# Attention and a gated feed-forward layer on one core: other costs in the kernel's own scheduler, loads held behind stores, and normalisations moved in pairs

## The chip, the cores and the metric

The kernel runs on one core of one Trainium2 chip. The metric is the device time of one execution in microseconds; the time of a kernel is the median of its runs. The engines are named as in the profile: PE (TensorE, matmuls), ACT (ScalarE), DVE (VectorE), POOL (GpSimd) and SP (SyncE). POOL and SP issue all the DMAs here: POOL the loads, SP the stores and the DMA transposes.

## The reference

Two steps, one behind the other. Inputs and output are float32.

```
k_proj = E @ k;  v_proj = F @ v            # per batch and head: 64 x 1024 times 1024 x 64
attn   = softmax(q @ k_proj.T / sqrt(64))  # 1024 x 64, over the 64 projected keys
x      = attn @ v_proj                     # 8 batches, 8 heads, 1024 tokens, 64 wide
x      = heads side by side                # 8192 tokens x 512
out    = (sigmoid(x @ w_gate) * (x @ w_val)) @ w_out   # 512 -> 1536 -> 512
```

## The kernel before

**Work.** A batch has 1024 tokens, and a block is half of that: 512 tokens, so there are 16 blocks. In a block the feed-forward layer runs in three units K (K = 3 times the block, plus 0 to 2), each over four of the twelve column groups of 128. Most matmuls are 128x128 by 256 columns in bf16: from block 1 on, products are taken by a scheme with seven instead of eight half-size products (the names S1 to S4 and T1 to T4 are its sums of activations and of weights). Sums of activations are made by `xs_sums` (L1627, out of xT) and `s_sums` (L1361, out of hT), sums of weights by `vt_sums` (L1555), `gt_sums` and `t_sums`. All these sums run on DVE.

**Buffers.** Eight PSUM banks (F0 to F3, A0 to A3). In SBUF there is one buffer for q of a batch (`Qb`), one for k and v (`KVs`), one for the turned q (`qT`), two for the turned attention output (`xT0`, `xT1`, by turns), two for the gated activations (`hT0`, `hT1`) and one for output rows (`ost`, four tiles of 128 rows). A buffer is used again as soon as its readers are done.

**Attention.** For batches 0 and 1 it is done with PE transposes and with softmax sums spread by matmuls. `bc2(R)` in batch 0 multiplies such spread reciprocals in PSUM, and the two normalisations behind it (`scale`, L825, on DVE) write the tokens of block 1 into xT. From batch 2 on, `head` (L1188) works on one head: scores, exponentials on ACT, the product with v, and `normal` on DVE. After every second head SP issues a DMA transpose of the pair into xT (L1217). q is turned in the same way into qT (L882, `transpose_q`), and the projected keys into kpB (L933). Each of these is a `DMA_TRANSPOSE` of SP.

**Order by hand.** Batch 0 (until about 86 us in the profile) is written out by hand: a list `todo` of PE steps, and extra pieces hung behind step i with `put(i, ...)` or, for the four parts of the later list, with `on(u, j, ...)`, which is `put(11 + 9u + j, ...)`. Steps 1 to 10 are the `mstep`s of block 0, four matmuls of 512 columns for the gate and four for the value, with a tanh on ACT and `gate` (L1287, its product is L1294) on DVE. Steps 11 and 13 are `g_step`s of block 1, step 12 (`p1`) and step 14 (`p26`) are its value products.

**Order by a scheduler.** All that follows (blocks 2 to 15, and with it batches 2 to 7 of the attention) is first noted as tasks and then put in order by `arranged` (L53). It goes through the tasks on a clock of its own. A task is ready when its predecessors are done by the counts of `COST` (L28): `busy` is how long a task keeps its engine, `lat` is how long until its result is there. Of the ready tasks of an engine, the one with the earliest due time (`rank`) goes first. The order it finds is the order in which each engine's queue holds its instructions; on the chip every engine then works through its queue strictly in that order, and stops at the first instruction whose semaphores are not there. A DMA counts as follows (L39):

```
if self.dma:
    self.busy, self.lat = (0.85 if eng == "POOL" else 0.6), t if t is not None else 3.0
```

So a load on POOL is counted with 26.0 to landing (`load`, L397), and every DMA of SP with 0.6 at issue and 3.0 to landing. A store has a further `pad` of 3.0 on each of its predecessors (L1452).

**Dependencies.** A task names keys that it reads (`r`) and writes (`w`). A reader waits for the last writer, a writer waits for the last writer and for all readers since. The same keys give the waits on the chip (`Plan.add`, L149) and the predecessors in the scheduler. A wait for a DMA is a wait for its landing.

**Loads.** In batch b (b = 1 to 6) `next_loads(b + 3)` (L2041) issues the loads of q, k and v of batch b + 3. They read the keys `("turned", r)`, so they wait for the four xT transposes of the batch; k also waits for kpB. In program order these loads come behind the stores of block 2b - 1 and ahead of those of block 2b.

**Stores.** `o_chain` (L1459) makes the output products of one block, evicts them into `ost` (`evac`, `add_snap`), and `stored` (L1443) issues one store of 256 KB per tile: tiles 2 and 3 first, then 0 and 1. The first eviction of a block (tiles 0 and 1, by ACT) overwrites what the last two stores of the block before it read.

Of the kernel before, what the change touches and what calls it, by code (L numbers as in the profile page):

```python
# [27 lines left out]
COST = {"PE": (0.0, 0.22), "ACT": (0.52, 0.12), "DVE": (0.63, 0.12), "SP": (0.1, 0.0), "POOL": (0.85, 0.0)}  # L28


class Task:
    def __init__(self, eng, call, t):
        self.eng, self.calls, self.goal = eng, [] if call is None else [call], None
        busy, tail = COST[eng]
        self.busy = busy if t is None else t
        self.tie, self.pad = (), 0.0
        self.lat = self.busy + tail
        self.dma = call is not None and call[5] is not None
        if self.dma:  # L39
            self.busy, self.lat = (0.85 if eng == "POOL" else 0.6), t if t is not None else 3.0  # L40

    def pre_of(self, later):
        return later.pre[self.n]
# [73 lines left out]
class Plan:  # L117
# [20 lines left out]
    @contextlib.contextmanager  # L138
    def group(self, goal, us):
        if self.tasks is None:  # L140
            yield
            return
        self.open = Task("PE", None, us)
        self.open.goal = goal
        yield
        self.tasks.append(self.open)
        self.open = None
# [85 lines left out]
def bass_linformer_attn__then__ffn_glu_sigmoid_kernel(  # L233
# [18 lines left out]
    with contextlib.ExitStack() as es:  # L252

        def sbuf(name, shape, dtype):
            return es.enter_context(nc.sbuf_tensor(name, shape, dtype))
# [8 lines left out]
        def within(shape, dtype):  # L264

            n = 1
            for x in shape[1:]:
                n *= x
            if dtype == FP32:
                n *= 2  # L270
            t = early[0][:, used[0] : used[0] + n]
            used[0] += n
            if dtype == FP32:
                t = t.bitcast(FP32)
            if len(shape) == 3:
                t = t.rearrange("p (a b) -> p a b", a=shape[1])
            if len(shape) == 4:
                t = t.rearrange("p (a b c) -> p a b c", a=shape[1], b=shape[2])
            return t
# [7 lines left out]
        kp = within([P, NR, DH], BF16)  # L287
# [21 lines left out]
        qT = sbuf("qT", [P, H, 512], BF16)  # L309
        eT = sbuf("eT", [P, 8, 512], BF16)  # L310
        xu = sbuf("xu", [P, 8, 512], FP32)
        xT = [sbuf(f"xT{i}", [P, NI, 2, 512], BF16) for i in range(2)]
# [59 lines left out]
        def mm(b, o, lhsT, rhs, r, start=True, stop=True, tp=None, tr=False, read=False):  # L372
            kw = {"skip_group_check": True} if read else {}
            if tp is not None:
                kw["tile_position"] = tp
            if tr:
                kw["is_transpose"] = True
            else:
                kw["start"], kw["stop"] = start, stop
            return add("PE", lambda e: e.matmul(o, lhsT, rhs, **kw), r=r, x=[("bank", b)])  # L380

        def act(o, i, r, w, b=None, func=AF.Copy, scale=1.0, t=None):
            x = [] if b is None else [("bank", b)]
            return add("ACT", lambda e: e.activation(o, i, func, scale=scale), r=r, w=w, x=x, t=t)  # L384
# [493 lines left out]
        def transpose_q(tie=(), rs=range(NR)):  # L878
            for r in rs:
                add(  # L880
                    "SP",
                    lambda e, r=r: e.dma_start_transpose(  # L882
                        qT[:, 2 * r : 2 * r + 2, :].rearrange("p h (t c) -> p (h t) c", c=P),
                        Qb[:, 2 * r : 2 * r + 2, :].rearrange("p h c -> p (h c)"),
                    ),
                    r=[("Q", hf, r // 2) for hf in range(2)],
                    w=[("qT", r)] + [("qT", hf, r // 2, r % 2) for hf in range(2)],
                    dma=f"qT{r}",
                    tie=tie,
                )  # L890

# [60 lines left out]
        def attention(b):  # L952
# [235 lines left out]
            def head(h, goal, gap, x0, x1):  # L1188
                with group(goal, 0.215):
                    mm(x0, bank[x0][:, :], kpB[:, h, :], qT[:, h, :], ["kpB", ("qT", h // 2)])  # L1190
                act(
                    eT[:, h, :],
                    bank[x0][:, :],
                    [],
                    [("eT", h)],
                    b=x0,
                    func=AF.Exp,
                    scale=SCALE,
                )
                with group(goal + gap, 0.23):  # L1200
                    for f, bk in ((1, x0), (0, x1)):
                        for k in range(2):
                            j = 2 * f + k
                            mm(
                                bk,
                                bank[bk][:, 130 * k : 130 * k + 130],
                                eT[:, h, 128 * j : 128 * j + 128],
                                vpB[b % 2][:, h, :],
                                [("eT", h), ("vpB", b % 2, 0), ("vpB", b % 2, 1)],
                            )  # L1210
                normal(h, 1, x0)
                normal(h, 0, x1)
                if h % 2:
                    r = h // 2
                    add(
                        "SP",
                        lambda e: e.dma_start_transpose(  # L1217
                            xT[s][:, r, :, :].rearrange("p f (n c) -> p (f n) c", c=P),
                            xk[:, r, :, :, :, :].rearrange("p f g k x -> p (f g k x)"),
                        ),  # L1220
                        r=[("xk", r, c, f) for c in range(2) for f in range(2)],
                        w=[("xT", s, r, f, g) for f in range(2) for g in range(2)]
                        + [("turned", r)],
                        dma=f"xT{r}",
                    )

            return dict(
# [215 lines left out]
        def stored(blk, tts):  # L1443
            for tt in tts:
                t = 2 * (2 * (blk % 2) + tt % 2) + tt // 2
                add(
                    "SP",
                    lambda e, tt=tt, t=t: e.dma_start(out_v[blk // 2, t], ost[:, tt, :]),
                    r=[("ost", tt, n) for n in range(2)],
                    dma=f"out{tt}",  # L1450
                    t=3.0,
                    pad=3.0,  # L1452
                )
# [101 lines left out]
        def vt_sums(n, part):  # L1555
            c0, c1 = ((0, 256), (256, DFF // 2))[part]
            js = ((0,), (1, 2))[part]
            B11 = wV[:, 0:2, c0:c1]
            B12 = wV[:, 0:2, DFF // 2 + c0 : DFF // 2 + c1]
            B21 = wV[:, 2:4, c0:c1]  # L1560
            B22 = wV[:, 2:4, DFF // 2 + c0 : DFF // 2 + c1]
            T = [vT[:, k, :, c0:c1] for k in range(3)]
            o, a, b = {
                3: (T[1], B22, B12),
                1: (B12, B12, B11),
                2: (T[0], T[1], B11),
                4: (T[2], B21, T[0]),
            }[n]
            w = [("vT", n, part)]
            if n == 1:  # L1570
                w += [("wV", 3 + j, 0) for j in js]
            else:
                w += ["bsel8f", "identf", "count", "pats"]
            r = [("wV", j + k, x) for j in js for k in (0, 3) for x in range(2)]
            if n == 1:
                r = [("wV", j, 0) for j in js]
            if n == 2:
                r = [("wV", j, 0) for j in js] + [("vT", 3, part)]
            if n == 4:
                r = [("wV", j, 1) for j in js] + [("vT", 2, part)]  # L1580
            op = ALU.add if n == 2 else ALU.subtract
            dve(lambda e: e.tensor_tensor(o, a, b, op), r, w)
# [334 lines left out]
        def put(i, fn):  # L1917
            at.setdefault(i, []).append(fn)
# [4 lines left out]
        def x_sums(blk, *ns):  # L1923
            return lambda: [xs_sums(blk, n) for n in ns]
# [5 lines left out]
        qt2, sc2, den2, bc2, xo2 = half_unit(1, att)  # L1930
# [1 line left out]
        put(4, lambda: (sc2(0), sc2(1)))  # L1932
        put(4, second_loads)
        put(6, lambda: (den2(), xo2(0), xo2(1)))
        put(8, lambda: (bc2(0)(), bc2(1)()))
        put(9, x_sums(1, 1, 2))
        put(7, lambda: (vt_sums(3, 0), vt_sums(2, 0)))
        put(8, lambda: (vt_sums(4, 0), vt_sums(1, 0)))

        def own_banks():  # L1940
            FF[:] = [ffn.next() for _ in range(4)]
# [25 lines left out]
        def on(u, j, fn):  # L1967
            put(11 + 9 * u + j, fn)

        on(0, 1, x_sums(1, 3))  # L1970
        on(0, 3, x_sums(1, 4))
        on(0, 3, lambda: vt_sums(3, 1))
        on(0, 4, lambda: vt_sums(2, 1))
# [66 lines left out]

        def next_loads(b):  # L2041
            done = [("turned", r) for r in range(NR)]
            if b < B:
                load_q(b, done)
                load_k(b, ["kpB"] + done)
                load_v(b, done)
# [65 lines left out]
```

## Time and profile before

| | |
|---|---|
| median of 10 runs | 521.82 us |
| lowest and highest | 520.62 and 527.47 us |
| the profiled execution | 522.0 us, span 520.0 us |
| granted PE clock in it | 0.999 |
| PE busy | 503.9 us, 97% |
| DVE, ACT busy | 407.8 us, 78%; 349.1 us, 67% |
| loads of q, k, v (1 MB each), median to landing | 20.4, 15.5, 13.6 us |
| stores out of ost (256 KB), median to landing | 2.5 us |
| DMA transposes into qT, xT, kpB, median to landing | 3.5, 3.1, 3.2 us |

The span is the time from the first to the last instruction of the program; the time of the execution has 2.0 us more around it. Busy time is how long an engine had an instruction in it. Matmuls are pipelined, so each is shown longer than the step from one to the next. In the timelines each row has its start and its length in microseconds, the engine, the line, the operation with output and inputs, how many such instructions in a row it stands for, and in square brackets how long the engine stood idle before it and what it waited for. "SPq" is SP's queue: a row there lasts from the issue of the first to the end of the issue of the last. A landing is the time at which the DMA's semaphore is complete.

### The profile page before, as it was taken

Reading aid. Unit: us, or ns where it says so; the run is one execution under the profiler, and the core shown is the slowest. Engines: PE = TensorE matmul, PEld = TensorE weight load, DVE = VectorE, ACT = ScalarE, POOL = GpSimd, SP = SyncE. Lnnn points to the kernel's source line nnn. Section 1 sums busy time; section 2 is a strip of 40 time slices with the busy share of each in tenths; the row PEclk is TensorE's granted clock in tenths of the full one; section 3 lists DMA queues with packets and bytes.
Section 4 is the critical chain, followed back from the end, with each engine's and each line's share of the span. In section 5 each row is a group of like instructions: output and inputs, shape, how many; then the busy total and the mean of one; then the engine's idle time right before and its main releaser. Section 6 shows DMA issues by size and latency. Waiting matters only on the chain.

```text
span 520.0 us, 11316 instructions
## 1 busy us (share of the span) xinstructions
PE 503.9 (97%) x4564; PEld 409.7 (79%) x4597; DVE 407.8 (78%) x802; ACT 349.1 (67%) x650; POOL 40.4 (8%) x59
## 2 busy tenths in 40 slices
PE   5999999999999999999999999999999999999996
PEld 2544545887888788887788888888888888888885
DVE  3547789899779795987769977797968898777774
ACT  2555683878677767777667686777777766676752
POOL 9420201200200010002000020000000000000000
PEclk9999999999999999999999999999999999999999
DMA  9999999899898496546926499344104330201013
GB/s 164 199 199 204 148 201 210 122 180 222 127 228 150 107 189 112 128 83 118 219 69 122 63 169 197 82 106 88 72 1 102 42 103 1 81 2 68 14 42 122
DMA packets 105189, 63.13 MB, mean 121 GB/s; under 512 B 63025, under 2 KB 97329, under 8 KB 105137
## 3 DMA queue, kind: packets, MB, share of 16 engines
q0 software_dynamic: 33984, 29.89, 37.3%
q1 hardware_dynamic: 71152, 32.52, 28.1%
q8 instruction: 36, 0.59, 0.5%
q14 instruction: 17, 0.13, 0.1%
HBM read 60.29 MB, written 16.78 MB: 148 GB/s over the span
## 4 chain that ended last, share of the span: by engine, by line
PE 91%; DVE 3%; DMA 3%; ACT 1%; issue 1%; POOL 0%; ACTq 0%; DVEq 0%; POOLq 0%
PE pA L380 49%; PE pF L380 42%; DMA Qb<-in_q_dram 2%; DVE hT L1824 1%; DMA xT<-xu 1%; DVE vsnap L1702 1%; DVE xT L828 0%; ACT vsnap L384 0%; DVE hT L1294 0%; POOL KVs L398 0%; DVE xS L1635 0%; ACT ost L384 0%; ACT kpd L384 0%; ACT sig L384 0%; DVE gT L776 0%
## 5 line engine op out<-in xcount | busy, mean ns | idle before, releaser
L384 ACT ACTIVATE sig<-pA 128x512 f32<-128x512 f32 x126 | 75.1, 596 | 45.3 <-PE pA L380 44.8
L1691 ACT ACTIVATE pF<-pA 128x512 f32<-128x512 f32 x99 | 58.3, 589 | 30.1 <-PE pA L380 27.5
L1702 DVE TENSOR_TENSOR vsnap<-pF,vsnap 128x512 f32<-128x512 f32 x90 | 61.8, 686 | 17.5 <-ACT vsnap L384 9.6
L1778 DVE TENSOR_TENSOR sig<-pF,sig 128x512 f32<-128x512 f32 x84 | 57.6, 686 | 5.7 <-PE pA L380 2.7
L380 PE MATMUL pF<-wO,hT 128*128 128x256 bf16 (+1 forms) x400 | 59.1, 285 | 0.5 <-issue 0.2
L1824 DVE SCALAR_TENSOR_TENSOR hT<-sig,vsnap 128x512 bf16<-128x512 f32 x84 | 56.3, 685 | 1.1
L384 ACT ACTIVATE sig<-sig 128x512 f32<-128x512 f32 x84 | 52.7, 627 | 5.6 <-DVE sig L1778 5.2
L380 PE MATMUL pF<-xS,wV 128*128 128x256 bf16 x360 | 54.1, 273 | 1.2 <-DVE hT L1824 0.7
L384 ACT ACTIVATE vsnap<-pA 128x512 f32<-128x512 f32 x84 | 50.0, 596 | 7.4 <-PE pA L380 7.0
L1824 DVE SCALAR_TENSOR_TENSOR hT<-sig,pF 128x512 bf16<-128x512 f32 x42 | 28.8, 685 | 31.6 <-PE pF L380 31.5
L380 PE MATMUL pA<-xT,gT 128*128 128x256 bf16 x336 | 50.5, 273 | 1.3 <-ACT sig L384 0.9
L380 PE MATMUL pA<-xT,vT 128*128 128x256 bf16 x336 | 50.4, 273 | 0.3
L380 PE MATMUL pF<-xS,wG 128*128 128x256 bf16 x336 | 50.4, 273 | 0.0
L380 PE MATMUL pF<-xT,wG 128*128 128x256 bf16 (+1 forms) x257 | 48.9, 309 | 1.5 <-DVE hT L1294 0.8
L384 ACT ACTIVATE sig<-pF 128x512 f32<-128x512 f32 x66 | 39.5, 598 | 14.6 <-PE pF L380 13.1
L380 PE MATMUL pA<-wT,hT 128*128 128x256 bf16 x360 | 48.8, 273 | 0.0
L380 PEld LDWEIGHTS pF<-wO,hT 128*128 128x128 bf16 x402 | 38.7, 98 | 10.6 <-issue 0.8
L380 PE MATMUL pF<-xT,wV 128*128 128x256 bf16 (+1 forms) x240 | 41.5, 294 | 0.2
L380 PEld LDWEIGHTS pF<-xS,wV 128*128 128x128 bf16 x360 | 34.4, 98 | 8.2 <-DVE vsnap L1702 1.6
L380 PEld LDWEIGHTS pA<-wT,hT 128*128 128x128 bf16 x360 | 34.6, 98 | 5.1 <-ACT EF L384 0.3
L384 ACT ACTIVATE eT<-pA 128x512 bf16<-128x512 f32 x59 | 34.5, 594 | 4.8 <-PE pA L380 3.6
L380 PEld LDWEIGHTS pA<-xT,gT 128*128 128x128 bf16 x336 | 31.0, 98 | 8.4 <-issue 1.9
(162 smaller groups left out, 899.8 us busy)
## 6 DMA issues: line engine op xcount, KB each, us to landing
out_dram<-ost SPq DMA_DIRECT2D x61, 256.0 KB, 2.5
Qb<-in_q_dram POOLq DMA_DIRECT2D x7, 1024.0 KB, 20.4
KVs<-in_k_dram POOLq DMA_DIRECT2D x7, 1024.0 KB, 15.5
KVs<-in_v_dram POOLq DMA_DIRECT2D x7, 1024.0 KB, 13.6
wO<-in_moe_w_out_dram POOLq DMA_DIRECT2D x1, 1536.0 KB, 12.3
wG<-in_moe_w_gate_dram POOLq DMA_DIRECT2D x5, 256.0 KB, 18.0
wV<-in_moe_w_val_dram POOLq DMA_DIRECT2D x5, 256.0 KB, 18.6
KVs<-in_k_dram POOLq DMA_DIRECT2D x2, 512.0 KB, 8.9
```

The lines of the kernel that those rows point to most:

```text
L380: return add("PE", lambda e: e.matmul(o, lhsT, rhs, **kw), r=r, x=[("bank", b)])
L384: return add("ACT", lambda e: e.activation(o, i, func, scale=scale), r=r, w=w, x=x, t=t)
L1691: lambda e: e.activation(bank[c][:, :], bank[a][:, :], AF.Copy, scale=1.0),
L1702: lambda e: e.tensor_tensor(o, bank[bk][:, :], o, ALU.add),
L1778: dve(lambda e: e.tensor_tensor(o, bank[bk][:, :], o, ALU.add), [key], [key], b=bk)
L1824: lambda e: e.scalar_tensor_tensor(o, sg.rearrange("p (j c) -> p j c", j=2), 1.0, x.rearrange("p (j c) -> p j c", j=2), ALU.add, ALU.mult,),
```

## The change

It has four parts.

1. In the scheduler's counts a DMA transpose of SP (the keys of its semaphores begin with xT, qT or kp) keeps SP for 1.3 instead of 0.6. A transpose into qT is counted with 4.5 to landing and one into xT with `TURN = 7.0`, each instead of 3.0; the one into kpB keeps its 3.0.
2. The stores in `stored` also write a key `("stored", tt)`.
3. The loads of batches 5, 6 and 7 also read these four keys, so they wait until the stores of the block in front have landed. By the rule of the keys, the stores of the next block in turn wait for these loads.
4. In batch 0 the normalisations `bc2(0)` and `bc2(1)` no longer stand together behind step 8: the second pair stands behind step 9. The sums `x_sums(1, 1, 2)` go from step 9 to step 10, `vt_sums(1, 0)` from step 8 to step 10 and `vt_sums(4, 0)` from step 8 to `on(0, 2)`, which is step 13.

```diff
+TURN = 7.0
...
         if self.dma:
             self.busy, self.lat = (0.85 if eng == "POOL" else 0.6), t if t is not None else 3.0
+            if eng == "SP" and call[5][:2] in ("xT", "qT", "kp"):
+                self.busy = 1.3
...
                     dma=f"qT{r}",
+                    t=4.5,
                     tie=tie,
...
                         dma=f"xT{r}",
+                        t=TURN,
...
                     r=[("ost", tt, n) for n in range(2)],
+                    w=[("stored", tt)],
                     dma=f"out{tt}",
                     t=3.0,
                     pad=3.0,
...
-        put(8, lambda: (bc2(0)(), bc2(1)()))
-        put(9, x_sums(1, 1, 2))
         put(7, lambda: (vt_sums(3, 0), vt_sums(2, 0)))
-        put(8, lambda: (vt_sums(4, 0), vt_sums(1, 0)))
+        put(8, lambda: bc2(0)())
+        put(9, lambda: bc2(1)())
+        put(10, x_sums(1, 1, 2))
+        put(10, lambda: vt_sums(1, 0))
...
         on(0, 1, x_sums(1, 3))
+        on(0, 2, lambda: vt_sums(4, 0))
...
             done = [("turned", r) for r in range(NR)]
+            if b > 4:
+                done += [("stored", tt) for tt in range(4)]
             if b < B:
                 load_q(b, done)
                 load_k(b, ["kpB"] + done)
```

## The prediction

> **What bounds the kernel now.** I read the page first, then the waits of TensorE (PE), then the timelines of the engines around each wait.
>
> ```profile
> span 520.0 us, 11316 instructions
> PE 503.9 (97%) x4564; PEld 409.7 (79%) x4597; DVE 407.8 (78%) x802; ACT 349.1 (67%) x650; POOL 40.4 (8%) x59
> PE pA L380 <- DMA EF<-in_F_dram: 5.8, 1, 5.8
> PE pA L380 <- ACT sig L384: 0.9, 1, 0.9
> PE pF L380 <- DVE hT L1294: 0.8, 1, 0.8
> PE pF L380 <- DVE hT L1824: 0.7, 1, 0.7
> ```
>
> PE is the bound, and the waits name nearly all that it loses: 5.8 us at the start, which the change doesn't touch, and three single waits. Here a rule of the Trainium skill speaks against such a reading. "Perfetto Trace Analysis", section "Identifying the Most-Contended Engine", says that matmul busy share tells little of the headroom because matmuls are pipelined, and that the weight-load share tells more; by that, 79% would leave some 100 us. The trace decides against it: in the timeline of PE four matmuls of 256 columns follow each other in 0.44 us (252.68, 253.12), 0.109 us each, batch after batch, although the group table gives one 273 ns. Starts back to back leave nothing between them. So the ceiling of any reordering is the sum of the waits, not 100 us. Counted by starts, the three are a little longer than the modelled ends show:
>
> ```profile
> 46.20 1.03 PE L380 MATMUL pF<-xT,wG 128*128 128x512 bf16 x3
> 47.32 0.61 PE L380 MATMUL pF<-xT,wV 128*128 128x256 bf16 x4
> 48.72 1.04 PE L380 MATMUL pF<-xT,wG 128*128 128x512 bf16 x4 [0.78 <-DVE hT L1294]
> ...
> 42.92 0.68 DVE L1294 SCALAR_TENSOR_TENSOR hT<-sig,pF 128x512 bf16<-128x512 f32 x1
> 43.52 2.48 DVE L828 TENSOR_TENSOR xT<-pA,xu 128x512 bf16<-128x512 f32 x4
> 45.91 0.41 DVE L1582 TENSOR_TENSOR vT<-wV,vT 128x512 bf16<-128x512 bf16 x1
> 46.25 0.42 DVE L1582 TENSOR_TENSOR wV<-wV 128x512 bf16<-128x512 bf16 x1
> 46.58 0.68 DVE L1294 SCALAR_TENSOR_TENSOR hT<-sig,pF 128x512 bf16<-128x512 f32 x1
> 47.98 0.68 DVE L1294 SCALAR_TENSOR_TENSOR hT<-sig,pF 128x512 bf16<-128x512 f32 x1
> ```
>
> Wait A. Four normalisations (2.48 us) and two weight sums stand on DVE between two gates (L1294). The gates free PSUM banks F2 and F0. PE's four 512-column matmuls from 46.20 take 0.87 and the next group comes at 47.32 (0.25 lost); its four of 0.109 end at 47.76 and the next comes at 48.72 (0.96 lost). A is 1.21 us.
>
> ```profile
> 122.54 2.06 SPq L882 DMA_TRANSPOSE qT<-Qb  x1
> 124.65 1.05 SPq L1448 DMA_DIRECT2D out_dram<-ost  x2
> 125.80 4.29 SPq L882 DMA_TRANSPOSE qT<-Qb  x3
> 130.18 1.44 SPq L933 DMA_TRANSPOSE xu<-kpd  x1
> 131.67 1.33 SPq L1217 DMA_TRANSPOSE xT<-xu  x1
> 134.94 0.43 DVE L1635 TENSOR_TENSOR xS<-xT 128x512 bf16<-128x512 bf16 x1 [1.81 <-DMA xT<-xu]
> 137.15 0.61 PE L380 MATMUL pF<-xS,wV 128*128 128x256 bf16 x4 [0.73 <-DVE hT L1824]
> ```
>
> Wait B. SP issues six transposes one behind the other, 1.3 to 2.1 us each; the scheduler had counted 0.6. The last xT lands at 134.8, while DVE already stands at the sums for the next batch: 1.81 us idle, and PE starts at 137.15 instead of 135.82 + 0.44. B is 0.89 us.
>
> ```profile
> 240.74 0.88 POOL L398 DMA_DIRECT2D KVs<-in_v_dram  x1 [57.17 <-PE pF L380]
> 242.36 0.88 POOL L398 DMA_DIRECT2D KVs<-in_k_dram  x1 [0.74 <-DMA xu<-kpd]
> out_dram<-ost SPq DMA_DIRECT2D x2, 256.0 KB, 9.1
> 253.08 0.60 ACT L384 ACTIVATE ost<-pF 128x512 f32<-128x512 f32 x1 [2.24 <-PE pF L380]
> 254.22 0.61 PE L380 MATMUL pA<-xT,gT 128*128 128x256 bf16 x4 [0.94 <-ACT sig L384]
> ```
>
> Wait C. The loads of batch 6 (1 MB each) start just ahead of block 5's last stores. Those land 9.1 us after issue (the pair two us earlier, 2.4). The eviction into the same ost rows stands still until 253.08: the named PE product was done by 251, so it is the store that came last. Starts give 254.22 - 252.68 - 0.44: C is 1.10 us. The same collision at 182 and 305 (7.6 us to landing) ended just in time.
>
> **The change part by part.** No instruction is added or removed; 3.2 us are at stake.
>
> *Normalisations in pairs.* bc2(0) stays behind step 9, bc2(1) goes behind step 10; two sums go later. PE has the same matmuls, eight of the sixteen one step later. DVE after the gate of step 9 (ends 43.52): two scales at 0.62 to 44.76, gate 10 to 45.4 instead of 47.2, two scales to about 46.65, gate 11 to 47.3 instead of 48.6. p1 at 47.1 finds F2 free, the next step at 47.6 finds F0 free. New: g_step(3,0) reads the second pair for i = 2 at 46.63, and it is ready at about 46.7, so 0.1 is lost there. The moved sums (0.42 each) come at 48.0 (T1, first used after 49) and 48.8 (T4, used later), inside the 1.43 us that DVE idled before 50.42. Gain 1.21 - 0.10 = 1.1 us. What is late next is wO: issued at 58.04 behind qT transposes that the loads pace, landing 12.3 later at 70.4, first read at 71.98, then at about 70.9. Cover 0.5 us; if gone, as much of A comes back.
>
> *Longer counts.* They alter only the order in which each engine's queue holds its work from 86 us on. With 1.3 per issue and 7.0 to landing, the scheduler puts the sums of wait B behind about 138 (an issue near 131 and 7.0), which a reader can set against the landing at 134.8; before, 3.0 gave it an earlier place than the chip could keep. Their consumers, batch 2's products, start near 147. So DVE goes on with gates and B's 0.89 goes. Here a second rule speaks against the change: "Advanced Engine Details and Errata", section "X-Bar Transpose (TRN2)", has transposes as fast as other DMAs, so one count for both would do. By the rows a store alone takes 2.2 to 2.5 and an xT alone 3.1 to 3.6, nearly the rule; but with loads beside it xT took 13.2 (98 to 108 us). By the rule the 7.0 is 4 us too long in quiet stretches, B stays and the sum ends at 520.0. I side with the issue rows above, since the lateness of B is the queue's (six issues of 1.3 and more), and what the excess costs is cover: xT of a batch lands near 302, needed near 330.
>
> *Loads behind stores.* Loads of batches 5, 6, 7 begin at about 185, 246 and 308 instead of 180, 241 and 304, 4 to 5 us later. POOL's queue holds nothing else there. Last landing 22 us after the first issue: 207, 268, 330. First readers: qT transposes at 210.6, 272.5, about 333; K and V are used 50 us later. If that 3 us of cover were gone, only qT for the next batch would slip, with some 50 us to spare. Stores now land in 2.4 us, ahead of 246, the eviction needs it at 251: C's 1.10 goes.
>
> A wait is added that the title doesn't tell. ("stored", tt) is read by the loads and written by the next stores, so those of blocks 4, 6 and 8 also wait until the loads have landed. In before block 4's go at 206.6 and 214.3: in real time 0.6 us at most. But the scheduler counts 26 us per load and a pad of 3: stores out at 188, loads at 189 to 191, landed at 216.6, next stores from 219.6. It will sort them behind qT(0), xT(0) and qT(1). Queued behind them on SP are the next transposes, with tens of us of slack; who waits is block 5's eviction into ost, now at 219.58 on ACT. The scheduler sees this and plans it near 223; its bank isn't wanted before about 227 (block 5's second snap is at 227.80). From below this costs nothing; from above, rival 2. I take nothing.
>
> *The new order itself.* No row shows it. Below: it could even shorten the end, where starts at 508.8 and 512.1 are 0.7 us late. Above: one more wait like the largest here, 1.1. The steady batches carry gaps near 0.2 by starts; I take two of these, +0.4.
>
> **Sum.** 522.0 (profiled execution, span 520.0 and 2.0 around it) - 1.1 - 0.9 - 1.1 + 0.4 = 519.3. The median of the runs, 521.82, is 0.2 below that execution: 519.1.
>
> **Rivals.**
> 1. *Gain spent elsewhere* (0.22). PE's order from 86 us on is greedy; two or three new waits near 0.9 take up what A, B and C give, or B stays because the sums wait on something else. For: such waits arise in single batches of one pattern. Against: batches 2 to 6 are nearly without waits under the same scheduler. 3.1 - 2.7: 521.4, between 520 and 522.5.
> 2. *The stores held by the loads' landing* (0.13), slower. If stores (0,1) of blocks 4, 6 and 8 leave SP at 219 to 220.5, they land at 222.8; an eviction still standing at 219.6 in ACT's queue waits 3.2. Wait C shows the exchange: 2.24 on ACT cost PE 1.10, so 1.1 is covered. 2.1 us three times, 6.3: 525.4. It decides from a landing over 1.1 us behind the eviction's place. For it: thin margins. Against: the scheduler knows the wait.
> 3. *The end improves too* (0.05): 519.1 - 0.7 = 518.4 and a little less.
> 4. *The main case* (0.60): 519.1, from 518.2 to 520.3.
>
> **Numbers.** About 0.5% (2.6 us, so 519.2) is what a measurement can tell. The main case lies across that bound: 0.45 of its 0.60 below, the rest within. Faster 0.45 + 0.05 = 0.50. Within: 0.15 and 0.18 of rival 1: 0.33. Slower: 0.13 and 0.04: 0.17. Range 517.8 to 522.8, which leaves out most of rival 2 and little below.
>
> **What would show it.** A: no wait of PE for L1294 near 47. B: no idle DVE before L1635 near 133. C: ost stores near 243 landing in under 3 us, loads behind them, ACT's eviction at 251. Wrong: PE waiting for ACT where ost evictions stand behind stores near 222, 284 or 345; new waits of PE by DVE or ACT over 0.5; a wait for wO near 71.

## The result, and the profile after

The kernel after the change takes 519.48 us, the median of 14 runs (518.51 to 520.35). The kernel before, run beside it, had a median of 522.64 in 51 runs, which scatter more (520.23 to 527.78, and one of 587.76), and the ratio is 0.9928 (95% interval 0.9904 to 0.9952). That is 3.8 us, with an interval of 2.5 to 5.0. The profiled execution took 519.21 us with a span of 517.4, at a granted clock of 1.0; the one before took 522.0 with 520.0. Single executions can also be compared stretch by stretch, because PE is almost never idle. For this I count from the start of the second 512-column gate matmul (it comes 21.7 to 23.1 us after the first instruction, whatever the kernel, and this jitter is left out so) to the start of the last matmul. I take the second because six of the fourteen traces, those of before and after among them, have no record of the first. That stretch was 494.06 us before and 491.39 after: 2.67 less.

```profile
span 517.4 us, 11347 instructions
PE 503.9 (97%) x4564; PEld 410.1 (79%) x4597; DVE 406.5 (79%) x802; ACT 348.2 (67%) x650; POOL 40.4 (8%) x59
```

These are the first lines of the page of the kernel after. PE has the same 503.9 us in the same 4564 records (the weight loads, 4597, show that 33 matmuls have none in either trace): nothing was made cheaper, waits went. The waits of PE after (total, count, longest) show which:

```profile
PE pA L385 <- DMA EF<-in_F_dram: 5.7, 1, 5.7
PE pF L385 <- issue: 0.5, 3, 0.2
PE pA L385 <- DMA Qb<-in_q_dram: 0.4, 1, 0.4
PE pA L385 <- DVE hS L1382: 0.3, 1, 0.3
```

The wait at the start stands, and the three single waits of 0.7 to 0.9 by ACT, by L1294 and by L1824 are no longer in the list. L385 is the line that was L380.

**Where wait A was.** The timeline of PE after:

```profile
42.42 0.40 PE L385 MATMUL pA<-wT 32*128 32x128 bf16 x8
42.75 1.04 PE L385 MATMUL pF<-xT,wG 128*128 128x512 bf16 x4
...
44.58 0.40 PE L385 MATMUL pA<-wT 32*128 32x128 bf16 x8
44.91 1.04 PE L385 MATMUL pF<-xT,wG 128*128 128x512 bf16 x4
...
46.65 1.03 PE L385 MATMUL pF<-xT,wG 128*128 128x512 bf16 x3
47.51 0.60 PE L385 MATMUL pF<-xT,wV 128*128 128x256 bf16 x4
47.95 1.03 PE L385 MATMUL pF<-xT,wG 128*128 128x512 bf16 x4
```

The groups at 46.65, 47.51 and 47.95 now follow each other by starts 0.86 and 0.44 apart: wait A is gone. But `bc2`, which was one group of sixteen small matmuls, is two groups of eight, and each holds PE for 0.33 (42.42 to 42.75, 44.58 to 44.91).

**Where wait B was.** SP, PE and DVE after:

```profile
129.36 1.23 SPq L1223 DMA_TRANSPOSE xT<-xu  x1
130.69 1.28 SPq L887 DMA_TRANSPOSE qT<-Qb  x1
132.06 1.29 SPq L939 DMA_TRANSPOSE xu<-kpd  x1
135.23 0.60 PE L385 MATMUL pA<-xT,vT 128*128 128x256 bf16 x4
135.67 0.60 PE L385 MATMUL pF<-xS,wV 128*128 128x256 bf16 x4
139.20 0.41 DVE L1643 TENSOR_TENSOR xS<-xT 128x512 bf16<-128x512 bf16 x1
```

The last xT is issued third from the end at 129.36 instead of last at 131.67, the sum that waited for it stands at 139.20 instead of 134.94, and PE's products with xS (of the batch before) follow without a gap.

**Where wait C was.** POOL's first load of batch 6, the last two stores ahead of it (issued within 241 to 243; KB each, median us to landing) and ACT's eviction after:

```profile
245.11 0.88 POOL L403 DMA_DIRECT2D Qb<-in_q_dram  x1 [57.89 <-PE pA L385]
out_dram<-ost SPq DMA_DIRECT2D x2, 256.0 KB, 2.3
249.50 0.60 ACT L389 ACTIVATE ost<-pF 128x512 f32<-128x512 f32 x1
```

The load is behind the stores, they land in 2.3 us, and the eviction stands in ACT's queue without a wait.

The saving by stretches, between the starts of the projection groups that PE runs once per batch (62.9, 152.3, 213.1, 274.9, 335.6 us after that gate matmul in the kernel before). Minus is less time than before:

| kernel | to 63 (A) | to 152 (B) | to 213 | to 275 (C) | to 336 | to the end | sum |
|---|---|---|---|---|---|---|---|
| after | -0.72 | -0.82 | -0.01 | -1.16 | +0.14 | -0.10 | -2.67 |
| counts only | -0.02 | -0.83 | -0.02 | -1.17 | -0.01 | -0.11 | -2.16 |
| loads only | -0.01 | -0.06 | -0.01 | -1.17 | +0.14 | -0.01 | -1.12 |
| pairs only | -0.72 | +0.31 | -0.02 | +0.34 | +0.20 | 0.00 | +0.11 |
| counts and pairs, no loads part | -0.65 | +0.33 | -0.01 | -1.17 | -0.01 | -0.12 | -1.63 |
| after, small matmuls together | -1.06 | -0.84 | -0.01 | -1.17 | +0.19 | -0.11 | -3.00 |

Each row is one profiled execution. To the first mark, executions of the same code agree within 0.1 us (six of the old code took 62.86 to 62.88). Behind it a wait that ends with a DMA's landing can differ by some tenths: the load of q for batch 3 took 22.0 to 24.6 us in the fourteen traces.

### The profile page after: what moved, and what is told of

Same layout as the page of the kernel before. It is cut to its first block, busy times and chain, and to the rows that moved or that the text cites. A ratio compares the mean times of both kernels' runs of the same rounds, so it can differ in the third digit from the quotient of the medians.

```text
span 517.4 us, 11347 instructions
## 1 busy us (share of the span) xinstructions
PE 503.9 (97%) x4564; PEld 410.1 (79%) x4597; DVE 406.5 (79%) x802; ACT 348.2 (67%) x650; POOL 40.4 (8%) x59
## 4 chain that ended last, share of the span: by engine, by line
PE 94%; DMA 2%; DVE 1%; issue 1%; ACT 1%; POOL 0%; ACTq 0%; POOLq 0%
PE pA L385 51%; PE pF L385 44%; DMA Qb<-in_q_dram 2%; DVE hT L1832 0%; POOL KVs L403 0%; DVE vsnap L1710 0%; ACT vsnap L389 0%; DVE gT L781 0%; ACT vpD L389 0%; DVE ost L1437 0%; ACT sig L389 0%; DVE sig L1786 0%; ACT qT L389 0%; ACT ost L389 0%; DVE vpD L683 0%
## 5 line engine op out<-in xcount | busy, mean ns | idle before, releaser
L385 PE MATMUL pF<-wO,hT 128*128 128x256 bf16 (+1 forms) x400 | 59.1, 285 | 0.5 <-issue 0.2
L385 PE MATMUL pF<-xS,wV 128*128 128x256 bf16 x360 | 54.1, 273 | 0.4
L385 PE MATMUL pA<-xT,gT 128*128 128x256 bf16 x336 | 50.5, 273 | 0.3
L385 PE MATMUL pA<-xT,vT 128*128 128x256 bf16 x336 | 50.4, 273 | 0.3
L385 PE MATMUL pF<-xS,wG 128*128 128x256 bf16 x336 | 50.4, 273 | 0.0
L385 PE MATMUL pF<-xT,wG 128*128 128x256 bf16 (+1 forms) x257 | 48.9, 310 | 0.7 <-issue 0.4
L385 PE MATMUL pA<-wT,hT 128*128 128x256 bf16 x360 | 48.8, 273 | 0.1
L385 PEld LDWEIGHTS pF<-wO,hT 128*128 128x128 bf16 x402 | 38.6, 98 | 10.5 <-issue 0.8
L385 PE MATMUL pF<-xT,wV 128*128 128x256 bf16 (+1 forms) x240 | 41.5, 294 | 0.0
L385 PEld LDWEIGHTS pF<-xS,wV 128*128 128x128 bf16 x360 | 34.6, 98 | 7.2 <-DVE vsnap L1710 1.5
L385 PEld LDWEIGHTS pA<-wT,hT 128*128 128x128 bf16 x360 | 34.5, 98 | 5.2 <-ACT EF L389 0.6
L385 PEld LDWEIGHTS pA<-xT,gT 128*128 128x128 bf16 x336 | 31.1, 98 | 7.5 <-issue 1.9
```

## The experiments

### Each part alone

`counts_only` is the kernel before with the first part of the change:

```diff
+            if eng == "SP" and call[5][:2] in ("xT", "qT", "kp"):
+                self.busy = 1.3
...
+                    t=4.5,
...
+                        t=7.0,
```

> The kernel before with the scheduler's longer counts alone (issue 1.3, landing 4.5 and 7.0). Theory (three separate waits that add up): wait B near 136 is gone, worth 0.8 to 0.9 us; wait A near 47 (PE for the gate) and wait C near 253 (ACT for an ost store) stay; profiled span about 519.2, ratio about 0.998. Rival (the new order as a whole brings the gain): two thirds of it here, 1.7 us or more, span 518.3 or less. Rival (the counts move waits about): B goes but PE waits of the same size come elsewhere, ratio 1.00.

Measured: 520.22 us (519.56 to 520.43, 5 runs), ratio 0.9967 (0.9954 to 0.9980); row two of the table. Wait A stays, wait B is gone, and so is wait C, which the prediction had given to the loads part. POOL and ACT of this kernel:

```profile
241.53 0.88 POOL L400 DMA_DIRECT2D KVs<-in_k_dram  x1 [57.94 <-PE pA L382]
242.39 0.89 POOL L400 DMA_DIRECT2D KVs<-in_v_dram  x1
250.25 0.60 ACT L386 ACTIVATE ost<-pF 128x512 f32<-128x512 f32 x1 [0.26 <-PE pA L382]
```

Before, v was first at 240.74; now k is, at 241.53. The last two stores of block 5 leave SP at 241.95 and 242.33. The first lands 2.5 us later, the second 7.9 us later, at 250.2 instead of 253.0, and ACT's wait is 0.26 instead of 2.24. The loads still collide with a store; the collision just ends in time. So the longer counts change POOL's order too, and through it wait C.

`loads_only` has only the third part (with the second, that it needs):

```diff
+                    w=[("stored", tt)],
...
+            if b > 4:
+                done += [("stored", tt) for tt in range(4)]
```

> The kernel before with the loads of batches 5 to 7 behind the stores alone. Theory: wait C goes, 1.1 us in the profile; A and B stay; span about 518.9. As the stores' landing beside loads varies from run to run and the collisions at 182 and 305 ended just in time, the median can gain more than the profile: ratio 0.996 to 0.998 and a narrower spread than before. Rival (stores held by the loads' landing): PE waits for ACT near 222, 284 and 345 take back 1 us or more, ratio 1.00 or over.

Measured: 521.17 us (520.10 to 521.72, 11 runs), ratio 0.9976 (0.9957 to 0.9995). In the table C is gone and A and B stay, as the prediction had it. Its waits of PE:

```profile
PE pF L380 <- DVE hT L1294: 0.8, 1, 0.8
PE pF L380 <- DVE hT L1825: 0.7, 1, 0.7
```

`pairs_only` has only the fourth part:

```diff
-        put(8, lambda: (bc2(0)(), bc2(1)()))
-        put(9, x_sums(1, 1, 2))
...
-        put(8, lambda: (vt_sums(4, 0), vt_sums(1, 0)))
+        put(8, lambda: bc2(0)())
+        put(9, lambda: bc2(1)())
+        put(10, x_sums(1, 1, 2))
+        put(10, lambda: vt_sums(1, 0))
...
+        on(0, 2, lambda: vt_sums(4, 0))
```

> The kernel before with the normalisations in pairs and the moved sums alone. Theory: the waits of PE for the gates near 47 go, but the second group of small matmuls costs two more changes of shape; the step of PE to batch 2's first k and v product (84.7 in before) comes 0.7 us earlier; B and C stay; span about 519.3, ratio 0.998 to 0.999. Rival (wO's landing gives the time back): the step to the output products comes no earlier, no gain at 84.7.

Measured: 521.54 us (520.34 to 526.12, 12 runs), ratio 1.0009 (0.9987 to 1.0031). PE stands 0.72 earlier at the first mark, and by the end nothing is left of it. The waits of PE and ACT's eviction near 253:

```profile
PE pA L383 <- ACT sig L387: 1.3, 1, 1.3
PE pF L383 <- DVE hT L1827: 1.0, 1, 1.0
253.08 0.60 ACT L387 ACTIVATE ost<-pF 128x512 f32<-128x512 f32 x1 [2.58 <-DMA out_dram<-ost]
```

Wait B, 0.7 by the waits before, is 1.0 here, and wait C, 0.9 before, is 1.3. The eviction starts at 253.08, to the hundredth where it stood before: PE came sooner, the store landed when it had landed before. The gain was lost in waits that end with a DMA. That such a landing keeps its time whatever is saved ahead of it is not shown: the first load and the last two stores had left 0.3 to 0.4 us sooner too (240.41, 242.63 and 243.00 instead of 240.74, 242.98 and 243.35), and the stores took longer by as much (9.0 and 10.0 us instead of 8.5 and 9.7), which in one profile can be scatter.

`no_loads` is the kernel after without the two edits of `loads_only`:

> The changed kernel without the loads behind stores (counts and pairs only). Theory (the counts already ease wait C, since they change the order of the three loads so that the first of them starts 0.8 us later; the pairs' gain then counts): span about 517.3, median 0.2 to 0.7 under the run with the counts alone (520.22). Rival (without the loads part the gain of the pairs is taken back at a store that lands late, as with the pairs alone): ACT stands before an ost eviction near 250, PE loses 0.3 us or more, span 517.8 or over.

Measured: 519.38 us (518.16 to 520.07, 9 runs), ratio 0.9936 (0.9911 to 0.9961), nearly the median of the kernel after. Its profiled execution was the slowest of the nine (520.07), and shows wait C gone without the loads part, but three waits between 95 and 134 us. One of them is a collision of stores with the loads of batch 3, which no part of the change touches:

```profile
128.37 0.60 ACT L389 ACTIVATE ost<-pF 128x512 f32<-128x512 f32 x1 [2.23 <-PE pA L385]
```

What follows: the three parts don't add up. Alone they give 2.16, 1.12 and -0.11; together 2.67. Beside the longer counts the loads part gives nothing that can be measured here, and in these profiles the pairs are worth something only once B and C are gone.

### Which of the two counts removes B

`issue_only` is the kernel before with `self.busy = 1.3` alone, `landing_only` the kernel before with `t=4.5` and `t=7.0` alone.

> The kernel before with the issue of a transpose counted as 1.3, landings as before. Theory of the prediction (the lateness of B is that of SP's queue): B near 136 is gone. Rival (the landing count moves the sums of DVE): B stays, 0.5 us or more. C: stays at about 1 us if the order of the loads is that of before.

> The kernel before with the landings counted as 4.5 and 7.0, the issue as before. Theory of the prediction: part of B stays, as six issues in a row are counted as 3.6 instead of 8. Rival: 7.0 alone puts the sums behind the landing, B is gone here too, and the two counts are each enough.

Measured, one run each: 520.89 us (stretch 1.26 shorter than before) and 519.81 us (2.26 shorter). B is gone in both, by 0.91 and 0.96. SP and DVE of `issue_only`:

```profile
129.64 1.34 SPq L1219 DMA_TRANSPOSE xT<-xu  x1
133.74 0.42 DVE L1637 TENSOR_TENSOR xS<-xT 128x512 bf16<-128x512 bf16 x1
```

and of `landing_only`:

```profile
129.61 1.28 SPq L934 DMA_TRANSPOSE xu<-kpd  x1
130.94 1.34 SPq L1218 DMA_TRANSPOSE xT<-xu  x1
137.85 0.42 DVE L1637 TENSOR_TENSOR xS<-xT 128x512 bf16<-128x512 bf16 x1
```

The first issues the transpose about 2 us earlier (129.64 instead of 131.67), so that it lands (133.10) ahead of the sum, which has hardly moved in DVE's order (133.74; before, DVE stood ready for it at 133.13). The second leaves it last in SP's queue and moves the sum almost 3 us back (137.85 instead of 134.94). Either is enough: B was not the queue's alone, as the prediction had it, but a transpose and its reader standing some 2 us too near to each other, and they can be drawn apart at either end.

C goes with the landing counts: with `landing_only` POOL has k first again (241.71) and the stretch to 275 is 1.17 shorter; with `issue_only` v stays first (239.99), ACT waits 1.69 and only 0.54 of C goes.

### Whether the order of the loads is what removes C

In the kernel before the load of k waits for kpB and v doesn't. `v_waits` gives v the same wait, which was meant to hold the first load back behind the stores and to leave all else:

```diff
-                load_v(b, done)
+                load_v(b, ["kpB"] + done)
```

> The kernel before, but the load of v also waits for the landing of kpB, so the first of the three loads starts about 1 us later; the orders of PE, ACT, DVE and SP are those of before. Theory (C is decided by how far the last ost store is issued behind the first load): the stores near 243 land earlier than 253.0, ACT's idle time before the eviction falls from 2.2 to under 1.2 us and PE's wait near 253 is nearly gone, span about 519, A and B stay. Rival (C needs the stores ahead of all loads): the stores land at 252 or later and C keeps over 0.7 us.

Measured: 521.56 us (521.13 to 522.84, 12 runs), ratio 0.9985 (0.9964 to 1.0006). The issue of the two last stores of block 5 in the kernel before, then POOL, ACT and the same stores here:

```profile
242.98 1.55 SPq L1448 DMA_DIRECT2D out_dram<-ost  x2
241.79 0.87 POOL L398 DMA_DIRECT2D Qb<-in_q_dram  x1 [57.54 <-PE pF L380]
253.56 0.60 ACT L384 ACTIVATE ost<-pF 128x512 f32<-128x512 f32 x1 [1.67 <-PE pA L380]
out_dram<-ost SPq DMA_DIRECT2D x2, 256.0 KB, 8.6
```

The edit did not do what it was for. q, which was third and does not wait for kpB, now went first, and as far ahead of the two stores as v before: 2.23 and 2.61 us in both kernels (242.98 and 243.35 behind 240.74; 244.02 and 244.40 behind 241.79). The stores took 8.1 and 9.1 us instead of 8.5 and 9.7, and C kept about half. The theory's lead was never made, so the run does not try it. Of the rival, the stores landed after 252 as it said, but C kept less than its 0.7.

The other traces go further. At the three collisions (near 181, 242 and 304 us), `unplanned` left out, the eight stores that were issued at most 0.45 us behind the first load landed in 2.3 to 2.7 us, the 32 that were issued 0.65 to 2.61 us behind it in 5.2 to 10.0, and those ahead of it in 2.0 to 3.0. Which array goes first hardly matters: 0.76 us behind v the stores took 5.20 and 5.25, 0.77 behind q 5.18. The loss of C in `counts_only` fits this: the load's lead over the last store shrinks from 2.61 to 0.80 us and its landing from 9.7 to 7.9, and the other store escapes at 0.43. That is a relation found in the traces; no run changed the lead alone, and why the step lies there is open. Why longer landings put k first was not tried either.

### What the pairs cost at the small matmuls

`joint` is the kernel after, but with the sixteen small matmuls of `bc2` in one group behind step 8 as before, and only the normalisations apart:

```diff
-        put(8, lambda: bc2(0)())
-        put(9, lambda: bc2(1)())
+        apart = []
+        put(8, lambda: apart.extend((bc2(0), bc2(1))))
+        put(8, lambda: apart[0]())
+        put(9, lambda: apart[1]())
```

> The changed kernel, but the sixteen small matmuls of both pairs stay together behind step 8 and only the normalisations stand apart. Theory (the split of the matmuls cost 0.3 to 0.4 us of wait A's 1.2): the step to the k and v product of batch 2 comes at 83.4 instead of 83.8, span about 517.1, 0.3 under the changed kernel. Rival (the gain of A was short because the second pair's normalisations came late for step 11): no change, 83.8 and 517.4.

Measured: 519.06 us (519.01 to 519.23, 5 runs), ratio 0.9946 (0.9934 to 0.9958). The timeline of PE:

```profile
42.68 0.42 PE L385 MATMUL pA<-wT 32*128 32x128 bf16 x16
43.03 1.04 PE L385 MATMUL pF<-xT,wG 128*128 128x512 bf16 x4
```

Sixteen take 0.35, eight took 0.33: the half group costs nearly as much as the whole one, so splitting it costs about 0.3. The profiles agree. To the first mark the three kernels with one group and normalisations apart (this and the two of the last section) took 61.82 to 61.90, the five with two groups 62.16 to 62.22, the six of the old code 62.86 to 62.88. By means that is 61.85, 62.17 and 62.87: moving the normalisations is worth 1.02, and splitting the matmuls gives 0.32 of it back.

### The stores that wait for the loads

Rival 2 said that the stores of blocks 4, 6 and 8, held by the loads, could stop the next evictions. In the kernel after SP and ACT show how near that came:

```profile
216.28 1.44 SPq L887 DMA_TRANSPOSE qT<-Qb  x1
217.81 2.02 SPq L1455 DMA_DIRECT2D out_dram<-ost  x4
343.56 0.60 ACT L389 ACTIVATE ost<-pF 128x512 f32<-128x512 f32 x1 [0.51 <-DMA out_dram<-ost]
```

The four stores of block 4 leave at 217.81, behind a qT as the prediction said, those of block 8 at 339.01; only the last of the three makes ACT wait, 0.51 us. `free_stores` is the kernel after with the stores freed of this wait, by keys that carry the block:

```diff
-                    w=[("stored", tt)],
+                    w=[("stored", blk, tt)],
...
-                done += [("stored", tt) for tt in range(4)]
+                done += [("stored", 2 * (b - 3) - 1, tt) for tt in range(4)]
```

> The changed kernel, but the stores of blocks 4, 6 and 8 no longer wait for the loads (each block has its own key), on the chip and in the scheduler. Theory (the added wait costs only the last trace of ACT time near 343, 0.13 us of PE): stores of block 4 go at about 205 again, the idle 0.5 us of ACT near 343 is gone, span about 517.3. Rival (held stores cost real time in many runs): median 0.5 us or more under the changed kernel's 519.5.

Measured: 519.92 us (519.49 to 520.17, 7 runs), ratio 0.9963 (0.9949 to 0.9977). The stores of block 4 begin at 205.87, twelve us sooner, the 0.14 in the stretch to 336 is gone, and the whole stretch is 491.20 against 491.39. The added wait cost 0.14 in one place and some 0.2 in sum. The medians do not show it (519.92 here, 519.48 for the kernel after), and the rival, half a microsecond or more, did not come.

`unplanned` is the kernel after with the waits on the chip, but with the scheduler blind to them:

```diff
-        r.update(c[2])
+        r.update(k for k in c[2] if k[0] != "stored")
```

(and the same for the keys that are written).

> The changed kernel, but the scheduler doesn't count the keys of the stores; on the chip all waits stay as they are. Theory (in real time the loads land before these stores are due, so only the scheduler's 26 us per load make it move anything): stores of block 4 at 205 to 207, PE as in the changed kernel, span 517.3 to 517.6. Rival (an unplanned wait blocks SP and with it the transposes and ACT): PE waits near 222, 283 or 343 of 0.5 us or more, span 518 or over.

Measured, one run: 566.74 us, 47.5 more in the stretch than the kernel after, more than either theory had. The scheduler now puts loads between the stores of one block, and each holds the next on the chip. POOL and ACT:

```profile
181.70 0.88 POOL L403 DMA_DIRECT2D KVs<-in_k_dram  x1 [41.33 <-PE pF L385]
192.91 0.88 POOL L403 DMA_DIRECT2D KVs<-in_v_dram  x1 [10.33 <-DMA out_dram<-ost]
204.31 0.88 POOL L403 DMA_DIRECT2D Qb<-in_q_dram  x1 [10.52 <-DMA out_dram<-ost]
203.89 0.60 ACT L389 ACTIVATE ost<-pF 128x512 f32<-128x512 f32 x1 [15.11 <-DMA out_dram<-ost]
```

k, then a store, then v, then a store, then q: each waits for the landing of the one in front. ACT waits 15.11, 14.65 and 15.41 us at the three places, and PE loses 14.15, 13.69 and 14.45 by starts, in every case 0.96 less. So rival 2's exchange was right (1.1 us of an eviction's wait is covered, it said; 0.96 was measured), and its danger is real. What kept it away is that the scheduler knows the wait.

The other 5.2 us are the clock: behind the three waits the same matmuls fall back by another 1.3, 2.7 and 1.3 us against the kernel after. Stretches of this kernel (from and to, us, busy PE, PEld, DVE, ACT, POOL, granted PE clock, DMA share, GB/s), and PE on both sides of the wait:

```profile
191.00:205.00 14.00, 0.05 (x1) 0.00 (x0) 1.19 (x3) 1.11 (x3) 1.56 (x2) 0.61 0.61 113
205.00:208.00 3.00, 2.97 (x15) 2.16 (x16) 0.97 (x2) 1.07 (x2) 0.19 (x1) 0.53 0.66 68
208.00:212.00 4.00, 4.00 (x39) 3.51 (x38) 1.95 (x4) 2.99 (x6) 0.00 (x0) 1.00 1.22 202
190.45 0.60 PE L385 MATMUL pF<-xS,wV 128*128 128x256 bf16 x4
205.03 1.04 PE L385 MATMUL pA<-xT,gT 128*128 128x256 bf16 x4 [13.98 <-ACT sig L389]
```

In the wait the granted clock falls to half (at 194.17; the 0.61 is the mean over the row), and it stays there for the first 2.8 us after it: 15 matmuls in 2.97 us, then 39 in 4.00.

### Both improvements together

`joint_free` is `joint` with the freed stores of `free_stores`, `joint_noloads` is `joint` without the loads part.

> The changed kernel with the small matmuls of both pairs together and with stores that do not wait for loads. Theory: both small terms add up, 0.3 and 0.1 us, span 517.0, median 518.9 to 519.1. Rival: equal to the run with the joint matmuls alone (519.06), since the wait near 343 is noise.

> Longer counts, joint matmuls and normalisations apart, without the loads behind stores. Theory (the counts already took wait C, so the loads part adds nothing on top): median 518.8 to 519.3, no wait over 0.3 us near 250. Rival (the loads part makes the time steady): a wider spread than the 0.3 us of the joint run, with single runs over 520, and a median of 519.5 or more.

Measured: 519.18 us (518.57 to 519.47, 6 runs), ratio 0.9948 (0.9930 to 0.9965), and 519.24 us (518.77 to 520.43, 6 runs), ratio 0.9954 (0.9937 to 0.9971). Neither is faster than `joint` by its median, and their stretches (490.93 and 490.98 against 491.06) are shorter by no more than 0.13. Without the loads part one run of six was over 520, as the rival expected, but the median stayed; six runs can't tell whether the loads part makes the time steadier. In `joint_noloads` ACT and PE near wait C:

```profile
250.41 0.60 ACT L389 ACTIVATE ost<-pF 128x512 f32<-128x512 f32 x1 [1.03 <-PE pF L385]
251.04 0.60 PE L385 MATMUL pF<-xS,wV 128*128 128x256 bf16 x4
251.55 0.61 PE L385 MATMUL pA<-xT,gT 128*128 128x256 bf16 x4
```

ACT waits 1.03 us for the landing and PE's next group comes 0.07 late (0.51 behind a group of 0.44): an eviction may stand about a microsecond here for nothing. `joint` has the lowest median of all, some 0.3 to 0.4 under the kernel after by both the median and the stretch. The two were not timed against each other with an interval, so that it is faster than the kernel after is likely, not shown.

## Why the prediction was right, and where it was not

The time came out right: 519.3 for the profiled execution against 519.21, 519.1 for the median against 519.48, the main case. (The prediction calls the steps by the number of their `mstep`, one above that in `put`.) Its reading that PE is the bound, and that the sum of its waits is the ceiling, held to the end: PE's busy time did not change by a tenth, and the gain is three waits. The terms fared less well than their sum.

- **A, 1.1.** The mechanism was right and the term too large: 0.72 in the profile after, 0.70 by the means of five executions. DVE's order came almost as worked out (gates at 44.76 and 46.92). The step that failed is "PE has the same matmuls, eight of the sixteen one step later": the same matmuls in two groups take 0.66 instead of 0.35. With one group the gain is 1.02 by means and 1.06 in the single profile of `joint`, which is nearly the number predicted.
- **B, 0.9.** The size was right (0.82). The reason was half of it. "The lateness of B is the queue's" made the issue count decide, but the landing count alone removes B as well, by moving the sum instead of the transpose. The rule that was weighed there (transposes as fast as other DMAs, so the longer landing is wrong) is not refuted as a statement on a quiet chip. What fails is the conclusion that the sum would then end at 520.0: a landing count is also a distance that the scheduler puts between a DMA and its reader, and 7.0 does its work though the xT that it is about landed in 3.2 us in `landing_only`.
- **C, 1.1.** The size was right (1.16) and the part was wrong. The prediction credited it to the loads held behind the stores. Those do remove it (`loads_only`), but the longer counts alone had removed it already, by another order of POOL's loads and a smaller lead of the first over the last store. "They alter only the order in which each engine's queue holds its work" stood in the text, and I followed it on DVE and SP and not on POOL.
- **The wait that the loads put on the stores, nothing.** Right: 0.14 at one of the three places. The order predicted on SP (behind qT, xT, qT) and the later evictions came so, within 2 us; the loads went at 184.58, 245.11 and 306.21 where 185, 246 and 308 were expected.
- **The new order itself, +0.4.** Too large: what the kernel after shows beside A, B and C is the +0.14 of that wait and -0.10 in the last stretch. Term A was 0.4 too large as well, on the other side, so the two errors cancelled. That is luck, not working.
- **The cover of wO, 0.5.** It landed at 70.44 and was first read at 71.32: it never came to be missed.
- **Rival 1** (the gain spent elsewhere) did not happen in the kernel after, but `pairs_only` is just that: 0.72 gained and, in its one profile, all of it taken back by waits that end with a DMA.
- **Rival 2** priced its exchange rightly, and `unplanned` shows how it would have looked. **Rival 3** gave 0.10 at the end instead of 0.7.

## What to carry to other kernels

A wait that ends with a DMA's landing can take back the work saved ahead of it, as in `pairs_only`. Look for such waits first, and don't add up the gains of parts that share one. A planner's cost for a DMA is at the same time the distance it puts between the DMA and its reader, and it moves every queue: follow a changed count on all of them. When a group of small matmuls is split, count what a group costs, not what a matmul costs. And count from a matmul that has a record in every trace that is compared: a missing first one shifts the count by 0.22 us here.

## What the runs showed of the hardware

- How long a store takes goes with how far a load got ahead of it, and in a step: 2.3 to 2.7 us up to a lead of 0.45, 5.2 to 10.0 from 0.65 on. In `counts_only`, of two stores of 256 KB issued 0.4 us apart behind the first of the 1 MB loads, one landed in 2.5 us and the other in 7.9. The Trainium skill ("DMA: Bandwidth & Descriptors", section "Issuing engines are not separate DMA queues") says that DMAs of all issuing engines run on the same 16 DMA engines and interleave. That these stores, issued by SP, slow down beside POOL's loads agrees with it; the step is not in that statement.
- A wait of PE of 14 us costs more than its length. After each of the three in `unplanned` PE ran at a granted clock of 0.5 for another 2.8, 5.5 and 2.8 us. At half speed that is a loss of 1.4, 2.8 and 1.4, together 5.6, and the waits themselves leave 5.2 us over. "TensorE: Matmul & The Clock Gate", Part 1, gives about 3.4 us of sustained work until the full clock returns, in a window that does not start with the work. The trace agrees as to the window: the clock changed at 194.17, 207.82, 269.26, 286.33, 347.77 and 361.42, whole multiples of 3.41 us apart. But 2.8 is less than 3.4: a window in which PE worked for 2.79 of its 3.41 us was enough twice (from 204.41 and 358.01), one with 2.14 (from 279.50) was not.
- Eight matmuls of 32 rows by 128 columns hold PE for 0.33 us and sixteen for 0.35.
